# Bringing the attention sums of segments 1 to 3 to token-major layout by DMA transposes instead of selector matmuls, with a new instruction order

## The chip, the cores and the metric

The kernel runs on one core of a Trainium2 chip. The metric is the device time of one execution in microseconds (us), lower is better. The engines are named as the profile names them: PE is TensorE's matmuls, PEld its weight loads, DVE VectorE, ACT ScalarE, POOL GpSimd, SP SyncE (which issues the DMAs that matter here).

## The reference

One transformer block on 2048 tokens of width 640. The attention has 32 heads of 20 and goes through four segments of 512 tokens. Within a segment it is causal softmax attention; from one segment to the next it carries a linear memory M with its normaliser z. A SiLU feed-forward of width 1728 follows. All inputs are bf16.

```python
for s in range(4):                               # L = 512 tokens each
    p     = softmax(qs @ ks.T * scale + causal)  # per head
    a_dot = p @ vs
    a_mem = (phi(qs) @ M) / (phi(qs) @ z + 1e-6) # phi(t) = t+1 if t > 0 else exp(t)
    o     = g * a_mem + (1 - g) * a_dot          # g = sigmoid(beta), per head
    M, z  = M + phi(ks).T @ vs, z + phi(ks).sum()
h   = x + concat(o) @ wo                         # x was normalised before wq, wk, wv
out = h + silu(layernorm(h) @ w1) @ w2
```

## The kernel before

The kernel is a list of tasks. A task names its engines, what it reads and writes, and emits instructions. A long string ORDER, found by a search outside the kernel, lists every task in sequence with its engine (`/A`, `/D`, `/G` for ScalarE, VectorE, GpSimd) and its buffer slots (`:0,1`). Every engine runs its own tasks in that order.

Four heads form a group; one group in one segment is a tick, so segments 1 to 3 have 24 ticks (numbers 8 to 31). A tick goes: scores by row-tiled matmuls (`qk`), exponentials on ScalarE (`e`), causal masks on GpSimd (`mk`), sums by column-tiled matmuls (`av`), evacuation with the head's gate (`oe`), token-major layout and memory part on TensorE (`tn`), normalisation on VectorE (`nm`), and the addition of the two halves on GpSimd (`ad`).

```python
def e_mask(eng):                       # mk: GpSimd
    for co in diag:
        v = pt[:, pta.slot, :, co:co + 128]
        fns.append(lambda e, v=v: e.affine_select(out=v, in_=v, ..., compare_op=ALU.is_ge, fill=0.0, ...))
# ... (cut)
def e_av(eng):                         # av: sums of four heads, column-tiled; row 20 of 32 is the denominator
    ... e.matmul(bank(po)[32*r:32*r+32, q0:hi], lhsT=Vx[...], rhs=pt[...], tile_position=(0, 32*r))
def e_ot(eng):                         # oe: oTs = sums * (1 - g)-term, head-major [4 x 32 rows, 512 tokens]
    o, i_ = oTs[:, ots.slot, lo:hi], bank(po)[:, lo:hi]
# ... (cut)
pp = G.alloc("ps", 2 if s else 1)      # two PSUM banks: sums in the first, memory part in the second
def e_tn(eng):
    for i in range(b0, b1):            # memory part, token-major
        for q, (c, m) in enumerate(bl):
            ... e.matmul(bank(pp, 1)[:, V4*i:V4*i+V4], lhsT=phiQ[:, c, 128*i:128*i+128], rhs=Mzb[:, m, :], ...)
    for i in range(b0, b1):            # selector: turns 128 tokens of oTs token-major
        fns.append(lambda e, i=i: e.matmul(bank(pp)[:, V4*i:V4*i+V4],
                   lhsT=oTs[:, ots.slot, 128*i:128*i+128], rhs=sel, start=True, stop=True))
# ... (cut)
def e_nm(eng):                         # both halves at once, on VectorE
    T.add(DV, ... tensor_tensor(out=r2, in0=v[:, :, :, DH], in1=epsg, op=ALU.add))
    T.add(DV, ... reciprocal(out=r2, in_=r2))
    T.add(DV, ... tensor_tensor(out=on, in0=v[:, :, :, 0:DH], in1=r2, op=ALU.mult))      # 640 wide
def e_ad(eng):                         # ad: GpSimd adds the halves into otok
    T.add(PO, ... tensor_tensor(out=o_dst, in0=on[.., 0, :], in1=on[.., 1, :], op=ALU.add))
```

A rule of the program decides which full-tiled matmul tasks are split into four column tiles, so that they need no change of tiling:

```python
t.cm = t.mode == "c" or t.mode == "F" and (before + behind in ("cc", "cr", "rc"))
```

The softmax here doesn't subtract the row's maximum and nothing guards it: scores larger than these inputs give would overflow.

## Time and profile before

Three runs took a median of 304.71 us (304.3 to 306.35). The profiled execution has a span of 306.1 us and a mean granted clock of 0.989. The lines that carry the argument are shown in the prediction below.

| GpSimd work before | us |
|---|---|
| causal masks, 128 instructions of 0.65 us | 83.2 |
| additions of the halves, 24 of 0.81 us | 19.5 |
| powers for the layernorms, 32 of one column, 0.58 us each | 18.6 |
| memory products, 15 of 0.65 us | 9.6 |
| rest | 12.6 |
| all, 47% of the span | 143.5 |

A row of groups reads: line, engine, operation, output<-input, shapes, count, then busy us and mean ns of one, then the idle time of the engine ahead of it. The masks lie between exponentials and sums, so TensorE depends on GpSimd although GpSimd is idle half the time.

### The profile page before, as it was taken

The page shows a single profiled execution, that of the slowest core. Times are in us where ns is not written, and L with a number is a line of the kernel's source. Part 1 is how long each engine was busy: PE and PEld are TensorE (multiplying, and loading weights), DVE is VectorE, ACT ScalarE, POOL GpSimd, SP SyncE. Part 2 cuts the span into 40 slices and gives each one's busy share as a digit, 9 for nine tenths or more (in the row PEclk, how much of TensorE's full clock was granted, in tenths as well). Part 3 has the DMA queues.
Part 4 walks back from the last instruction along what each step waited for, and adds up shares of the span by engine and source line. Part 5 has one row for each costly group of instructions (what it writes and reads, how often), then busy time and mean ns, then how long its engine had stood idle before and what let it go on. Part 6 is the DMA issues. An engine that isn't in the chain of part 4 may idle for free.

```text
span 306.1 us, 8438 instructions
## 1 busy us (share of the span) xinstructions
PE 291.2 (95%) x3520; PEld 171.2 (56%) x3544; DVE 226.1 (74%) x496; ACT 220.0 (72%) x233; POOL 143.5 (47%) x280
## 2 busy tenths in 40 slices
PE   8989789999999999999999999999999999999996
PEld 6445435546665455576653544546665556764574
DVE  6677767898599896879998978886764696634623
ACT  4689959899989898995899798879768831003500
POOL 6145746375558766281736638464675530300000
PEclk9999879999999999999999999999999999999999
DMA  7949675660455111242433410144052014131002
GB/s 217 329 122 212 141 209 173 120 76 5 76 92 76 22 41 42 39 92 57 88 71 108 78 24 2 21 89 75 5 59 32 2 30 101 46 83 66 0 24 86
DMA packets 48581, 24.72 MB, mean 81 GB/s; under 512 B 38880, under 2 KB 47456, under 8 KB 48544
## 3 DMA queue, kind: packets, MB, share of 16 engines
q1 hardware_dynamic: 48544, 24.19, 35.5%
q8 instruction: 28, 0.46, 0.6%
q14 instruction: 9, 0.07, 0.1%
HBM read 10.41 MB, written 2.62 MB: 43 GB/s over the span
## 4 chain that ended last, share of the span: by engine, by line
PE 66%; DVE 14%; ACT 9%; DMA 6%; issue 3%; SPq 2%; ACTq 0%
PE ps_all L530 44%; PE ps_all L532 8%; PE ps_all L896 6%; PE ps_all L942 4%; DMA beta_bc<-in_A_beta_dram 4%; ACT PTA L907 3%; ACT PTB L907 2%; ACT PTE L907 2%; DMA x_tok<-in_A_x_dram 2%; DVE stt L720 2%; DVE on L1008 2%; PE ps_all L971 2%; DVE phiQ L849 1%; PE ps_all L975 1%; DVE sT L1176 1%
## 5 line engine op out<-in xcount | busy, mean ns | idle before, releaser
L907 ACT ACTIVATE PTA<-ps_all 128x2048 bf16<-128x2048 f32 x32 | 60.1, 1878 | 4.5 <-PE ps_all L896 4.2
L907 ACT ACTIVATE PTB<-ps_all 128x2048 bf16<-128x2048 f32 (+1 forms) x32 | 56.6, 1770 | 8.6 <-PE ps_all L896 8.5
L1170 ACT ACTIVATE th<-ps_all 128x512 f32<-128x512 f32 (+2 forms) x70 | 33.3, 501 | 39.0 <-PE ps_all L530 29.6
L919 POOL TENSOR_SCALAR_AFFINE_SELECT PTB<-PTB 128x512 bf16<-128x512 bf16 x64 | 41.3, 646 | 39.4 <-ACT PTB L907 37.1
L530 PE MATMUL ps_all<-w_sb,sT 128*128 128x320 bf16 x400 | 57.7, 299 | 0.5 <-DVE x_tok L1133 0.5
L530 PE MATMUL ps_all<-hT,w_sb 128*128 128x512 bf16 (+1 forms) x281 | 53.7, 338 | 1.1 <-DVE sT L1176 0.4
L1176 DVE SCALAR_TENSOR_TENSOR sT<-th,ps_all 128x512 bf16<-128x512 f32 (+2 forms) x70 | 37.8, 558 | 21.0 <-ACT th L1170 19.9
L530 PEld LDWEIGHTS ps_all<-w_sb,sT 128*128 128x128 bf16 x400 | 37.9, 98 | 17.6 <-issue 1.7
L530 PEld LDWEIGHTS ps_all<-hT,w_sb 128*128 128x128 bf16 x290 | 27.2, 98 | 22.9 <-issue 1.6
L907 ACT ACTIVATE PTE<-ps_all 128x2048 bf16<-128x2048 f32 (+1 forms) x20 | 34.1, 1707 | 6.4 <-PE ps_all L896 6.0
L919 POOL TENSOR_SCALAR_AFFINE_SELECT PTE<-PTE 128x512 bf16<-128x512 bf16 x40 | 26.2, 654 | 17.7 <-ACT PTE L907 16.3
L720 DVE BATCH_NORM_STATS2 stt<-x_tok 128x6 f32<-128x320 bf16 x64 | 27.8, 475 | 3.8 <-DMA x_tok<-in_A_x_dram 3.7
L1016 POOL TENSOR_TENSOR otok<-on 128x320 bf16<-128x320 bf16 x24 | 19.5, 812 | 18.7 <-DVE on L1008 18.7
L833 DVE CAST QK<-ps_all 128x512 bf16<-128x512 f32 x29 | 19.7, 686 | 8.8 <-PE ps_all L530 7.4
L1209 DVE SCALAR_TENSOR_TENSOR x_tok<-ps_all,x_tok 128x640 bf16<-128x640 f32 (+1 forms) x17 | 13.1, 780 | 12.8 <-PE ps_all L530 12.7
L896 PE MATMUL ps_all<-QK 20*128 20x256 bf16 (+3 forms) x360 | 20.5, 286 | 2.0 <-ACT PTE L907 1.3
L729 POOL TENSOR_TENSOR rst<-mvt,eps_c 128x1 f32<-128x1 f32 x32 | 6.5, 202 | 33.8 <-DVE mvt L723 33.8
L530 PE MATMUL ps_all<-xT,wqr 128*128 128x512 bf16 (+1 forms) x87 | 20.9, 368 | 0.9 <-issue 0.6
L919 POOL TENSOR_SCALAR_AFFINE_SELECT PTA<-PTA 128x512 bf16<-128x512 bf16 x24 | 15.7, 657 | 11.2 <-ACT PTA L907 10.9
L1008 DVE TENSOR_TENSOR on<-ps_all,rd 128x640 bf16<-128x640 f32 x24 | 19.8, 824 | 0.8
L530 PE MATMUL ps_all<-xT,wkr 128*128 128x512 bf16 x73 | 19.1, 394 | 1.1 <-issue 0.5
L731 POOL TENSOR_TENSOR rst<-rst,eps_c 128x1 f32<-128x1 f32 x32 | 18.6, 580 | 2.5
(92 smaller groups left out, 462.8 us busy)
## 6 DMA issues: line engine op xcount, KB each, us to landing
out_dram<-x_tok SPq DMA_DIRECT2D x15, 160.0 KB, 1.9
w_sb<-in_B_w_dram SPq DMA_DIRECT2D x5, 432.0 KB, 5.4
x_tok<-in_A_x_dram SPq DMA_DIRECT2D x3, 640.0 KB, 10.8
w_sb<-in_B_w_dram SPq DMA_DIRECT2D x3, 480.0 KB, 5.1
QKV<-QK SPq DMA_DIRECT2D x16, 72.0 KB
sT<-in_A_wq_dram SPq DMA_DIRECT2D x1, 800.0 KB, 5.9
sT<-in_A_wk_dram SPq DMA_DIRECT2D x1, 800.0 KB, 7.7
wv_sb<-in_A_wv_dram SPq DMA_DIRECT2D x1, 800.0 KB, 9.2
```

The lines of the kernel that those rows point to most:

```text
L530: return [lambda e: e.matmul(out(), lhsT=lhsT(), rhs=rhs(), start=start, stop=stop)]
L532: return [lambda e, r=r: e.matmul(out()[m * r:m * r + m, :], lhsT=lhsT()[:, m * r:m * r + m], rhs=rhs(), start=start, stop=stop, tile_posi ...
L720: T.add(DV, lambda e, hh=hh: e.bn_stats(out=stt[:, s, 6 * hh:6 * hh + 6], in_=xb[:, 320 * hh:320 * hh + 320]), reads=R((xa, xsub)), writes ...
L731: T.add(PO, lambda e: e.tensor_tensor(out=rst[:, s, :], in0=rst[:, s, :], in1=eps_c[:, 1:2], op=ALU.pow), reads=R((st, ["r"]), (C, ["half" ...
L833: (lambda e: e.tensor_copy(out=o, in_=i_))
L896: fns.append(lambda e, j=j, o=o, r=r, q0=q0, q1=q1, qa=qa, ka=ka: e.matmul(ps_all[:, o:o + q1 - q0], lhsT=ka[32 * r:32 * r + DH, 128 * j:1 ...
L907: T.add(AC, lambda e: e.activation(out=pt[:, pta.slot, q0:q0 + 4, 0:width], in_=sc3[:, b0:b0 + 4, 0:width], func=ACT.Exp, scale=SCALE), re ...
L919: fns.append(lambda e, v=v: e.affine_select(out=v, in_=v, pattern=[[0, 4], [1, 128]], compare_op=ALU.is_ge, fill=0.0, base=0, channel_mult ...
L1008: T.add(DV, lambda e: e.tensor_tensor(out=on[:, ona.slot, :, :].rearrange("p b (x e) -> p b x e", e=DH), in0=v[:, :, :, 0:DH], in1=r2.unsq ...
L1016: T.add(PO, lambda e: e.tensor_tensor(out=o_dst, in0=on[:, ona.slot, 0, :].rearrange("p (i x) -> p i x", i=4), in1=on[:, ona.slot, 1, :].r ...
L1170: T.add(AC, lambda e: e.activation(out=th[:, tha.slot, lo:hi], in_=bank(ps)[:, lo:hi], func=ACT.Tanh, scale=0.5), reads=R((ps, [0])), writ ...
L1176: T.add(DV, lambda e: e.scalar_tensor_tensor(out=sT[:, f, lo:hi], in0=th[:, tha.slot, lo:hi], scalar=1.0, in1=bank(ps)[:, lo:hi], op0=ALU. ...
```

## The change

The intent is to take 96 selector matmuls off TensorE, which is busy for 95% of the span. In segments 1 to 3 the evacuated sums go through a DMA transpose into a new tile `oto`. The memory part keeps one PSUM bank. The normalisation is halved, and the attention half becomes a task `nl` of its own: 13 of them are put on VectorE, 11 on GpSimd, which has no reciprocal task in this kernel and uses a power of -1. The column rule goes. ORDER is new throughout.

```diff
-            t.cm = t.mode == "c" or t.mode == "F" and (before + behind in ("cc", "cr", "rc"))
+            t.cm = t.mode == "c"
 ...
-            pp = G.alloc("ps", 2 if s else 1)
+            pp = G.alloc("ps", 1)
+            if s:
+                ota = G.alloc("oto")                                   # two buffers
+                dma(f"td{tag}", [(ots, [0])], [(ota, [0])],
+                    lambda e: e.dma_start_transpose(out=oto[:, ota.slot, :, :], in_=oTs[:, ots.slot, :]), ...)
 ...
-                for i in range(b0, b1):
-                    fns.append(... e.matmul(bank(pp)[...], lhsT=oTs[...], rhs=sel, ...))
+                    if not s:
+                        fns.append(... e.matmul(bank(pp)[...], lhsT=oTs[...], rhs=sel, ...))
 ...                                       # nm: the same three operations on the memory half only (16, 16, 320 wide)
+                def e_nl(eng):
+                    v = oto[:, ota.slot, :, :].rearrange("p i (r e) -> p (i r) e", e=32)
+                    if eng == DV:
+                        T.add(DV, lambda e: e.reciprocal(out=r2(0), in_=v[:, :, DH]), ...)
+                    else:
+                        T.add(PO, lambda e: e.tensor_tensor(out=r2(0), in0=v[:, :, DH],
+                                      in1=eps_c[:, 2:3].to_broadcast([128, 16]), op=ALU.pow), ...)
+                    T.add(eng, lambda e: e.tensor_tensor(out=o2(0), in0=v[:, :, 0:DH], in1=r2(0)..., op=ALU.mult), ...)
+                G.task(f"nl{tag}", {DV: 0.25 + dve_c(320), PO: 1.5}, e_nl, ...)
 ...
-zpad:0 mt1 mta1 iota mt3 halfc sel warm:0 mt2 mtb1 vpad0 x0:0 x1:1 ...      (ORDER, cut: some 90 lines)
+zpad:0 iota mt3 x0:0 x1:1 x2:2 x3:3 w_q:0 w_k w_wv:0 beta mt2 sel vpad0 ...
```

The number `PO: 1.5` is the duration in us that the program gives to the attention half on GpSimd.

## The prediction

> **What bounds the kernel now.** I read four views, in this order: the page's shares of the engines and its slices, the chain that ended last, the windows, and the matmul engine's timeline. First the shares, and the slices with the granted clock:
>
> ```profile
> PE 291.2 (95%) x3520; PEld 171.2 (56%) x3544; DVE 226.1 (74%) x496; ACT 220.0 (72%) x233; POOL 143.5 (47%) x280
> ...
> PE   8989789999999999999999999999999999999996
> ...
> PEclk9999879999999999999999999999999999999999
> ```
>
> TensorE is busy for 95% of the span; the two sevens and eights of its row are in slices 0 to 5, that is in segment 0, where the clock also dips. Then the chain:
>
> ```profile
> PE 66%; DVE 14%; ACT 9%; DMA 6%; issue 3%; SPq 2%; ACTq 0%
> ```
>
> Two thirds of it is TensorE, the rest short visits to other engines. So a matmul taken away counts nearly in full, and a microsecond on VectorE mostly doesn't. But busy time hides pauses, because the modelled ends of matmuls overlap. So I went to starts, in the timeline of TensorE:
>
> ```profile
> 146.02 0.39 PE L942 MATMUL ps_all<-PTB,Vx 128*32 128x384 bf16 x8
> 146.24 0.72 PE L532 MATMUL ps_all<-hT,w_sb 128*32 128x256 bf16 x20
> ...
> 151.54 0.31 PE L971 MATMUL ps_all<-Mzb,phiQ 128*128 128x84 bf16 x4
> 151.70 0.32 PE L975 MATMUL ps_all<-ident,oTs 128*128 128x84 bf16 x4
> 151.95 0.40 PE L896 MATMUL ps_all<-QK 20*128 20x384 bf16 x8
> 152.28 2.08 PE L530 MATMUL ps_all<-w_sb,sT 128*128 128x320 bf16 x14
> ```
>
> Three tilings alternate: full (128*128), column (128*32), row (20*128). Four memory matmuls start 0.16 us before the four selector matmuls behind them: 0.040 us each. The selectors then take 0.16 us, yet the row-tiled scores start only at 151.95, 0.09 us later: the price of a change of tiling. Column work followed by column work (146.02 to 146.24) pays nothing: (384+128)/2400 is 0.213 us. Over all 186 places where one matmul record and the next differ in tiling, the pause above streaming time has a median of 0.09 to 0.10 us, in each of the six directions.
>
> From this a budget of the 306.1 us profiled: streaming (columns at 2.4 GHz, four concurrent tiles counted once, small ones at 0.040) 263 us; 186 changes at 0.097, 18 us; 1.1 us before the first matmul and 3 us after the last; that leaves 21 us of waiting and half clock. By place, summing the excess between starts: about 3.4 us in the first 12 us, 7.9 between 12 and 60 (segment 0) and 10.7 in all the rest.
>
> **What the Trainium skill says.** "TensorE: Matmul & The Clock Gate", section "Back-to-back issue gap", gives N/2.4 + 2.5 ns between warm matmuls; the trace agrees, with a median of 2.5 ns above N/2.4 over 1,427 full-tiled pairs. "TensorEngine Tiling (Array Packing)", section "Key Properties", says that a change of tiling mode drains the engine; it states no price, the trace has 0.09 to 0.10 us. The first page's section "The HAM clock gate" says that an idle window of about 3.4 us halves the clock. The windows of one us each agree, with two half-clock stretches of 3.4 us:
>
> ```profile
> 35.00:36.00 1.00, 0.18 (x8) 0.00 (x0) 0.96 (x4) 1.00 (x2) 0.93 (x2) 0.88 0.53 97
> 36.00:37.00 1.00, 0.79 (x16) 0.56 (x20) 0.97 (x2) 1.00 (x2) 0.93 (x3) 0.50 0.55 104
> ...
> 43.00:44.00 1.00, 0.89 (x3) 0.34 (x3) 0.97 (x5) 1.00 (x1) 0.64 (x1) 0.50 1.04 379
> 44.00:45.00 1.00, 1.00 (x7) 0.16 (x9) 0.45 (x3) 0.72 (x2) 0.67 (x2) 0.50 1.07 394
> ```
>
> After window and length, the columns are the five engines, then the clock: 0.50 follows thin work. "DMA: Bandwidth & Descriptors", section "Anatomy of one DMA", says that a small transfer costs about 2 us, mostly completion; the page has 2.6 to 2.9 us from issue to landing for the transposes here.
>
> **The change part by part.** (a) In segments 1 to 3 the attention sum no longer goes through the selector. These rows tell the costs:
>
> ```profile
> L1008 DVE TENSOR_TENSOR on<-ps_all,rd 128x640 bf16<-128x640 f32 x24 | 19.8, 824 | 0.8
> ...
> L975 PE MATMUL ps_all<-ident,oTs 128*128 128x84 bf16 x128 | 11.4, 206 | 0.1
> ...
> L1007 DVE RECIPROCAL rd<-rd 128x32 f32<-128x32 f32 x24 | 8.5, 353 | 0.8
> ...
> L1002 DVE TENSOR_TENSOR rd<-ps_all,epsg 128x32 f32<-128x32 f32 x24 | 4.4, 184 | 7.8 <-PE ps_all L975 7.7
> ```
>
> Of the 128 selectors 32 belong to segment 0 and stay; 24 ticks of 4 go: 96 x 0.040 = 3.8 us of the bound. (The row's 206 ns is latency; 96 times that would be 20 us, and wrong.)
>
> (b) VectorE: a tick's normalisation was 184 + 353 + 824 = 1.36 us, 24 times 32.7 us. Half as wide it is, by my estimate from these rows and from the 320-wide PSUM read of 492 ns in the last block, 0.17 + 0.25 + 0.49 = 0.91 us, 21.8 us in all. The attention half is a new task, 13 times on VectorE at an estimated 0.25 + 0.43 us (8.8 us) and 11 times on GpSimd, whose power of one column takes 580 ns and whose 320-wide operation takes 812 ns in the trace: some 1.6 us each, 18 us. So VectorE falls by 2 us, GpSimd rises by 18 us to about 160.
>
> (c) SyncE issues 24 more transposes at about 1.25 us, 30 us on a queue that is now free for more than half of the span. In return the sum's second PSUM bank is free, and the memory matmuls no longer wait for the evacuation.
>
> (d) The rule that let a full matmul between two tiled tasks run as four column tiles is gone: 28 tasks had it. Counting tilings along the new order I get 214 changes against 186: 28 x 0.097 = 2.7 us more. This takes back most of (a). A full-tiled task itself streams at the same rate either way (ten of 320 columns take 1.37 us in both forms).
>
> (e) The new order of segment 0. It has 29 filler matmuls after the opening against 7: 2.4 us, meant for time when TensorE waits anyway. It should keep the clock up. A dip of 3.4 us costs at most 1.7 us. The first dip (36 to 39.4) is followed by a wait for the head copies until 40.4, so I count nothing for it; the second (42.6 to 46) is on the chain, 1.7 us. The warm-up of ScalarE moves from the empty start into the first scores, where 1.27 us may show.
>
> Sum: 304.7 - 3.8 + 2.7 - 1.7 = 301.9. I take another 1.2 us off for waits shortened by the free bank, the lighter VectorE and the search; this is a choice, some 6% of the 18.6 us of excess after the opening.
>
> **The rivals.** First, the exchange of tilings eats everything and segment 0 stays as it is: 304.7 - 3.8 + 2.7 = 303.6. For it: the changes are counted, while what the order gains is unknown. Second, the transposes make a new wait: evacuation, issue, 2.6 us, normalisation, addition in place of a matmul of 0.16 us; with two buffers each for the sums and their transposes, late ones hold the next evacuation and its PSUM bank. Against it: a tick comes only every 6 us or so, and the new order has nine other matmul tasks between the last sums and the last output projection. If it happened half a us in each of ten ticks, 306. Third, GpSimd becomes the bound where masks are dense: it is busy 5.6 of 6 us in one window already, though 47% on average; 1 to 3 us, 302 to 304. Fourth, waits and dips of segment 0 go almost wholly (up to 5 of its 7.9 us) and a quarter of the later 10.7 with them: 304.7 - 1.1 - 5 - 2.5 = 296.
>
> **Range and chances.** Predicted 300.7 us; 297.0 to 304.6 should hold it 8 times in 10. 2% faster is 298.6, which needs a gain of 6 us where the counted parts give 2.8; I give it 0.2. Slower by 2% needs the second rival at its worst: 0.03. Within 2%: 0.77.
>
> **What would show each step right or wrong.** The selector's row with 32 instances, not 128, and no column-tiled row of line 532. The pauses at changes of tiling summing to about 2.7 us more. A granted clock of 0.50 nowhere after the opening, or one stretch at most. Landing times of the new transposes near 2.7 us, and few waits of TensorE for evacuations of the sums. VectorE at about 224 us, GpSimd near 160. The prediction is wrong if the clock still dips, if the pauses don't grow by count, or if the excess in segments 1 to 3 moves by more than 3 us either way.

## The result

Three runs of the changed kernel took a median of 324.39 us (323.14 to 326.35). The ratio to before is 1.0639, with a 95% interval of 1.0535 to 1.0744. Ratios here are the mean time of one kernel's fast runs over that of the other's of the same rounds, so not quite the ratio of the medians. The kernel is 6.4% slower, outside the predicted range. The profiled spans are 322.2 and 306.1 us, with granted clocks of 0.984 and 0.989.

The page of the changed kernel: shares of the engines, TensorE by slices, granted clock by slices, chain that ended last.

```profile
PE 293.1 (91%) x2867; PEld 166.4 (52%) x2891; DVE 219.7 (68%) x523; ACT 219.3 (68%) x232; POOL 182.1 (57%) x303
...
PE   7899888999999498799989999699998979999996
...
PEclk9999999999999879999999999899999999999999
...
PE 52%; POOL 21%; DVE 10%; DMA 7%; ACT 6%; issue 3%; SPq 1%; ACTq 0%; DVEq 0%; POOLq 0%
```

VectorE fell by 6 us. GpSimd rose by 38.6 us, more than twice what was expected, and it holds 21% of the chain, in which it had no entry before. Apart from the last slice, TensorE's row has its lowest values in slices 13 and 25 (counted from 0), in segments 1 and 2, and the clock dips there and just behind. In segment 0 the clock has no dip left in this profile.

The groups of instructions, with shapes kept apart:

```profile
L1029 POOL TENSOR_TENSOR rd<-oto,eps_c 128x16 f32<-128x16 bf16 x11 | 32.1, 2916 | 0.0
...
L734 POOL TENSOR_TENSOR rst<-rst,eps_c 128x1 f32<-128x1 f32 x32 | 18.0, 564 | 2.5
...
L1017 DVE TENSOR_TENSOR on<-ps_all,rd 128x320 bf16<-128x320 f32 x24 | 11.8, 491 | 4.7 <-POOL otok L1039 4.0
...
L1032 POOL TENSOR_TENSOR on<-oto,rd 128x320 bf16<-128x320 bf16 x11 | 8.0, 727 | 0.9
...
L984 PE MATMUL ps_all<-ident,oTs 128*128 128x84 bf16 x32 | 3.6, 209 | 0.0
```

The first two rows are the same operation, a power (of -1 from bf16 in the first, of -0.5 from f32 in the second). One column takes 564 ns; sixteen columns take 2916 ns. The attention half on GpSimd is therefore 2.916 + 0.727 = 3.64 us, and eleven of them 40 us. The last row is the selector of segment 0, with its 32 instances.

Next the timeline of TensorE in the first bad place (start, duration, then in brackets the idle time before and the releaser):

```profile
106.17 0.33 PE L980 MATMUL ps_all<-Mzb,phiQ 128*128 128x84 bf16 x4
106.33 1.24 PE L532 MATMUL ps_all<-xT,wqr 128*128 128x512 bf16 x5
107.41 0.32 PE L980 MATMUL ps_all<-Mzb,phiQ 128*128 128x84 bf16 x4
112.03 0.62 PE L945 MATMUL ps_all<-PTA,Vx 128*32 128x512 bf16 x4 [4.30 <-DVE phiQ L849]
```

TensorE stands still for 4.30 us ahead of a tick's sums, and then runs them at half clock: 0.62 us for four tiles of 512 columns, where 0.40 us was usual a little earlier. The profile names a VectorE operation as the releaser. By the program these sums read Vx and the masked exponentials, and no phiQ. So I looked at the chain in that stretch (start, duration, what):

```profile
99.56 2.95 POOL rd L1029
102.52 0.07 issue
102.58 0.73 POOL on L1032
103.31 0.55 POOL Mzb L1123
103.86 0.79 POOL PTE L922
...
105.33 2.88 POOL rd L1029
...
108.28 0.73 POOL on L1032
109.01 0.74 POOL otok L1039
109.75 0.60 POOL PTB L922
...
111.04 1.48 POOL PTA L922 x2
```

GpSimd works without a gap: a power, a product, a memory product, masks, another power, product, addition, and only then the masks of PTB and PTA. These are what the waiting sums read. Of the two PTA masks only the first is of this tick: by the view of tile PTA it starts at 111.0 and takes 0.885 us, so it ends at about 111.9, and the weight load of the waiting sums starts at 112.00 (the second mask is of the next tick). The exponentials of this PTA had left ScalarE by 105.57. The windows, first of before, then of after, put the engines side by side; after window and length come PE, PEld, DVE, ACT, POOL, the clock, the DMA share and GB/s:

```profile
108.00:114.00 6.00, 5.69 (x80) 3.11 (x70) 5.93 (x11) 5.38 (x6) 3.62 (x7) 1.00 0.19 52
```

```profile
108.00:114.00 6.00, 1.97 (x25) 0.80 (x26) 3.50 (x8) 0.75 (x3) 5.78 (x10) 0.73 0.13 26
114.00:120.00 6.00, 5.78 (x39) 3.24 (x42) 2.49 (x6) 3.78 (x3) 5.92 (x7) 0.70 0.11 22
```

In the stretch from 108 to 114, TensorE falls from 5.69 to 1.97 us of work, ScalarE from 5.38 to 0.75 and VectorE from 5.93 to 3.50, while GpSimd rises from 3.62 to 5.78 of 6. A second place is at 204 us, with a wait of 3.10 us before 206.63. There the chain goes through two powers and the additions behind them to VectorE's normalisation, which TensorE waits for, and not through masks.

### The profile page after: what moved, and what is told of

Same layout as the page of the kernel before. It is cut to its first block, busy times and chain, and to the rows that moved or that the text cites. A ratio compares the mean times of both kernels' runs of the same rounds, so it can differ in the third digit from the quotient of the medians.

```text
span 322.2 us, 7230 instructions
## 1 busy us (share of the span) xinstructions
PE 293.1 (91%) x2867; PEld 166.4 (52%) x2891; DVE 219.7 (68%) x523; ACT 219.3 (68%) x232; POOL 182.1 (57%) x303
## 4 chain that ended last, share of the span: by engine, by line
PE 52%; POOL 21%; DVE 10%; DMA 7%; ACT 6%; issue 3%; SPq 1%; ACTq 0%; DVEq 0%; POOLq 0%
PE ps_all L532 42%; POOL rd L1029 9%; PE ps_all L899 5%; POOL PTB L922 3%; PE ps_all L945 3%; DMA oT<-otok 3%; POOL otok L1039 3%; DMA sT<-in_A_wk_dram 3%; POOL on L1032 2%; POOL PTA L922 2%; ACT PTB L910 2%; DVE on L1032 1%; ACT PTE L910 1%; DVE sT L1199 1%; DMA QKV<-QK 1%
## 5 line engine op out<-in xcount | busy, mean ns | idle before, releaser
L532 PE MATMUL ps_all<-w_sb,sT 128*128 128x320 bf16 x448 | 65.0, 299 | 0.8 <-DVE sT L1199 0.8
L532 PE MATMUL ps_all<-hT,w_sb 128*128 128x512 bf16 (+1 forms) x314 | 60.9, 335 | 3.0 <-DVE on L1017 1.5
L532 PEld LDWEIGHTS ps_all<-w_sb,sT 128*128 128x128 bf16 x448 | 42.6, 98 | 20.2 <-issue 2.0
L532 PEld LDWEIGHTS ps_all<-hT,w_sb 128*128 128x128 bf16 x325 | 29.5, 98 | 27.0 <-issue 2.6
L1029 POOL TENSOR_TENSOR rd<-oto,eps_c 128x16 f32<-128x16 bf16 x11 | 32.1, 2916 | 0.0
L532 PE MATMUL ps_all<-xT,wkr 128*128 128x512 bf16 x94 | 24.6, 398 | 4.2 <-DVE on L1017 3.1
L836 DVE CAST QK<-ps_all 128x512 bf16<-128x512 f32 (+1 forms) x30 | 19.9, 665 | 9.4 <-PE ps_all L532 9.2
L532 PE MATMUL ps_all<-wv_sb,xT 128*128 128x320 bf16 x160 | 26.1, 314 | 0.2
L532 PE MATMUL ps_all<-wo_sb,oT 128*128 128x320 bf16 x160 | 23.9, 300 | 2.0 <-DVE phiK L849 1.2
L945 PE MATMUL ps_all<-PTA,Vx 128*32 128x512 bf16 (+1 forms) x160 | 13.1, 350 | 9.5 <-DVE phiQ L849 4.3
```

The lines of the kernel that those rows point to most:

```text
L532: return [lambda e: e.matmul(out(), lhsT=lhsT(), rhs=rhs(), start=start, stop=stop)]
L836: (lambda e: e.tensor_copy(out=o, in_=i_))
L945: fns.append(lambda e, j=j, r=r, h=h, pa=pa, pt=pt, co=co, q0=q0, ji=ji: e.matmul(bank(po)[32 * r:32 * r + 32, q0:hi], lhsT=Vx[:, vx.slot, ...
L1029: T.add(PO, lambda e: e.tensor_tensor(out=r2(0), in0=v[:, :, DH], in1=eps_c[:, 2:3].to_broadcast([128, 16]), op=ALU.pow), reads=R((ota, [0 ...
```

## The experiments

Seventeen runs were made of sixteen kernels (one ran twice), in five calls; each call has its own runs of before, with medians of 306.84, 306.31, 306.11, 305.92 and 306.58 us. These are 1 to 2 us above the 304.71 that forecasts in us were worked out from, so ratios are what to compare. The theory: the power on GpSimd is the cause, by its length and by what queues behind it. The rivals: the detour of the sums through the DMA; the lost column rule; and the new order itself.

### Which part of the attention half

**All attention halves on VectorE.** Only the engine letter in ORDER changes, 11 times.

```diff
-nl8/G:0,0 nm8 mb02:0 mk12e v20:6 e12b0:1 nl9/G:1,1 ...
+nl8/D:0,0 nm8 mb02:0 mk12e v20:6 e12b0:1 nl9/D:1,1 ...
```

> The changed kernel with all 24 attention halves (reciprocal and product) on VectorE; the eleven powers of GpSimd are gone, the order is the same. Theory P (the power of 16 columns on GpSimd takes 2.91 us, not the 0.58 us of one column, and holds up masks and sums behind it): GpSimd falls by 11 x (2.91 + 0.73) = 40 us to about 142, VectorE rises by 11 x 0.74 = 8 us, no wait of TensorE over 2 us after segment 0, and the time comes to 301 to 306 us. Rival D (the detour through the DMA transposes is itself the new wait): the long waits stay and the time stays within 3 us of 324. Rival T (more changes of tiling, or the new order as such): the same, 320 or more.

Correct; median 315.96 us, ratio 1.0306 (1.0267 to 1.0345). VectorE rises to 228.6 us busy and 17% of the chain, GpSimd falls to 145.0. Half of the loss is gone, the other half is not, and neither forecast held (301 to 306 us for the power, 320 or more for the rivals). That the halves now wait in VectorE's queue, and other work behind them, would fit, but no run isolates it.

**A multiplication in place of the power.** Wrong results; the same operands, the same place.

```diff
-    in1=eps_c[:, 2:3].to_broadcast([128, 16]), op=ALU.pow),
+    in1=eps_c[:, 2:3].to_broadcast([128, 16]), op=ALU.mult),
```

> The changed kernel with a multiplication in place of the power, on the same engine, place and shape; the values come out wrong on purpose. Theory P: the 16-column instruction falls from 2.91 us to about 0.25, GpSimd by 11 x 2.65 = 29 us to about 153, and the time to 302 to 307 us: it is the function, not the place, that costs. If GpSimd is too slow for these halves whatever the function (rival G), the time stays above 312. Rivals D and T: within 3 us of 324.

Median 308.87 us, ratio 1.0084 (1.0039 to 1.0129). From 1.0639, this is 5.5 points, some 17 us, from one operation code in eleven instructions. Its shares, and the row of `oto` with minimum, median and maximum in ns:

```profile
PE 292.8 (95%) x2891; PEld 165.8 (54%) x2891; DVE 222.9 (72%) x523; ACT 219.7 (71%) x232; POOL 154.1 (50%) x303
```

```profile
L1029 POOL TENSOR_TENSOR rd<-oto,eps_c x11: 213/220/229, 99.2 to 243.1; 128x16 f32<-128x16 bf16 x11
```

In the changed kernel the same row reads:

```profile
L1029 POOL TENSOR_TENSOR rd<-oto,eps_c x11: 2899/2907/2995, 99.5 to 254.1; 128x16 f32<-128x16 bf16 x11
```

The multiplication takes 0.220 us where the power has a median of 2.907, and GpSimd's share of the chain falls from 21% to 1%. So it is neither the width nor the strided bf16 input that costs, but the power. In this trace the sums that waited until 112.03 start at 107.15, with 0.8 us of the difference already there at the tick before (100.34 against 101.12), and in the window at 108 all engines are busy again:

```profile
108.00:114.00 6.00, 4.95 (x48) 2.76 (x44) 5.83 (x13) 5.07 (x5) 5.41 (x10) 1.00 0.52 49
```

**The reciprocal on VectorE, the product where it was.** A correct kernel without the power.

```diff
+ def e_nr(eng):   # new task nr, VectorE
+     T.add(DV, lambda e: e.reciprocal(out=r2(0), in_=v[:, :, DH]), ...)
- nl11/G:3,1
+ nr11:3 nl11/G:1
```

> The changed kernel with all 24 reciprocals on VectorE and the eleven products left on GpSimd; results are right. Theory P: like the multiplication for the power, 302 to 307 us, with GpSimd at about 182 - 32 = 150 us and VectorE 11 x 0.25 = 3 us up. Rivals D and T: within 3 us of 324.

Correct; 311.54 us, ratio 1.0178 (1.0127 to 1.0228). **The same kernel again**, on another chip, as a base for others:

> The kernel of the run with reciprocals on VectorE, word for word, measured again with more rounds, as the measure for the two runs that were built on it (tilings back: 1.0228; no fillers: 1.0240). If it comes to 1.016 to 1.020, both edits made it slower by about 0.5%; if it comes to 1.022 or more, neither did anything.

Correct; 312.85 us, ratio 1.0227 (1.0182 to 1.0271). Both times are above the forecast of 302 to 307 us, also when it is moved up by the 1 to 2 us by which before ran slower here. This is the best correct form of the changed program that I found, and still slower than before. It is a point or so above the multiplication; that GpSimd's products now wait for VectorE's queue would fit, but no run isolates it.

**Two powers of 8 columns.** Is the cost per instruction or per column?

```diff
+ for q in range(2):
+     T.add(PO, ... tensor_tensor(out=r2(0)[:, 8*q:8*q+8], in0=v[:, 8*q:8*q+8, DH], in1=..[128, 8], op=ALU.pow))
```

> The changed kernel with each power of 16 columns cut into two of 8. If the power costs by column (a line through 0.565 us for 1 column and 2.907 for 16: 0.41 + 0.156 a column), one of 8 takes 1.66 us and the span grows by up to 11 x 0.4 us, to 322 to 328. If it costs by instruction, each takes 2.9 us and the span is 335 us or more. If columns are handled in groups of 16, 2.9 us each too.

Correct; one time of 333.07 us, state unknown, so the time decides nothing. The row does:

```profile
L1030 POOL TENSOR_TENSOR rd<-oto,eps_c x22: 1632/1640/1731, 100.9 to 264.1; 128x8 f32<-128x8 bf16 x22
```

8 columns take 1.640 us and 16 take 2.907: 0.158 us a column and 0.37 us once. That puts one column at 0.53 us; 0.564 is measured, for the power of -0.5 from f32. A line of 0.41 + 0.156 per column meets all three to 0.02 us.

### The detour through the DMA

**No wait for the transposes.** On top of the multiplication, the halves read a constant tile of ones; the transposes are still issued. Wrong results.

```diff
-                    v = oto[:, ota.slot, :, :].rearrange("p i (r e) -> p (i r) e", e=32)
+                    v = ones[:, :, :].rearrange("p i (r e) -> p (i r) e", e=32)
```

> The kernel with a multiplication for the power (1.0084 of before), whose attention halves read a tile of ones in place of the transposed sums; the transposes are still issued, but no engine waits for their data. Values are wrong on purpose. Rival D (what is left of the loss is waiting for the 24 transposes): 0.985 to 0.998 of before. Theory O (what is left is the new order itself, with its changes of tiling and fillers): 1.004 to 1.012, as without the edit.

307.91 us, ratio 1.0057 (1.0015 to 1.01), against 1.0084 with the wait. The intervals overlap: in the new order the wait costs 0.8 us at most likely, and perhaps nothing. In the changed kernel the transposes land in a median of 2.5 us.

**The old order with the change in it.** Before, with its ORDER and its column rule; the transpose is put right behind the evacuation, the halves on VectorE ahead of the additions, four buffers for `oto`.

```diff
-mzc8 ad9 mb03:0 h2_1_2 av11:3 qk13a0:4 oe11/A:0 h2_1_3 ... oe10/D:1
+mzc8 nl9/D ad9 mb03:0 h2_1_2 av11:3 qk13a0:4 oe11/A:0 td11:3 h2_1_3 ... oe10/D:1 td10:2
```

> The order and the tiling rule of the kernel before, with only the token-major attention sum: transposes right behind the evacuations, reciprocal and product of all 24 ticks on VectorE just ahead of the addition, four buffers for the transposed sums. TensorE loses 96 selectors (3.8 us), VectorE gains 24 x (0.74 - 0.46) = 6.8 us. Theory P+order (the power and the new order made the loss; the idea is sound): 0.985 to 0.998 of before. Rival D (the detour itself costs): VectorE stands still for transposes and the ratio is 1.01 or more.

Correct; 363.07 us, ratio 1.1851 (1.1796 to 1.1906). A far larger loss than expected. **The same with the products on GpSimd** (`nl9/D` becomes `nr9 nl9/G`):

> Like the old order with the token-major sum, but with all 24 products on GpSimd (0.73 us each, 17.5 us) and only the reciprocals (0.25 us) on VectorE, which so loses 24 x (1.36 - 0.91 - 0.25) = 5 us. Theory P+order: 0.985 to 1.000 of before, and better than all on VectorE if VectorE is what the short waits of TensorE are for. Rival G (GpSimd too full, masks wait behind products): 1.01 or more.

Correct; 362.87 us, ratio 1.1855 (1.1802 to 1.1909). Which of the two engines does the products makes no difference here. The waits of SyncE in the first of the two (line waited for, us in total, times, longest) led on:

```profile
SPq L971 <- ACT oTs L959: 32.4, 6, 11.6
SPq L971 <- DVE oTs L961: 31.1, 4, 14.2
```

SyncE stands for 63.5 us with a transpose in hand whose evacuation has not come. Its timeline shows what that holds up:

```profile
242.49 1.21 SPq L1141 DMA_TRANSPOSE oT<-otok  x1
253.19 1.19 SPq L971 DMA_TRANSPOSE oto<-oTs  x1
254.43 1.41 SPq L864 DMA_DIRECT2D QKV<-QK  x2
255.88 2.51 SPq L1080 DMA_TRANSPOSE phiKt<-phiK  x2
258.44 2.82 SPq L864 DMA_DIRECT2D QKV<-QK  x4
```

From 243.70 to 253.19 nothing is issued; then one transpose of sums, and behind it eight other transfers in one go. They belong to other work: head copies for the scores, transposes for the memory. The transposes of the output (`oT`) are issued from the same queue; in one line of the program alone the matmuls of this trace wait 11.8 us for them and the weight loads 12.8.

**The old order, transposes later.** Each `td` is moved some ten tasks back, with its halves and additions.

```diff
-... oe10/D:1 td10:2 o1 qk12a0:4 e12a0:1 tn10:0 qe200/D:0 v20:2 qk12b0:4 mb04:0 mk13a mk12a nm10:2,0 ...
+... oe10/D:1 o1 qk12a0:4 e12a0:1 tn10:0 qe200/D:0 td11:2 v20:2 qk12b0:4 mb04:0 mk13a mk12a td10:3 nm10:2,0 ...
```

> The old order with the token-major sum on VectorE (1.185 of before), with one edit: each of the 24 transposes stands about ten tasks later in SyncE's queue, and the half and the addition later where they stood within 20 tasks of it. Theory H (SyncE's queue is in order, and a transpose that waits for its evacuation holds up the head copies and the transposes of the output behind it): SyncE's waits at the new transposes fall from over 60 us to under 30, TensorE's waits for transposed outputs from 24 us to under 6, and the ratio to 0.99 to 1.06. If the old order can't take the detour for another reason (buffers, VectorE standing still): above 1.12.

Correct; 340.78 us, ratio 1.1134 (1.1082 to 1.1186). The later place of 24 issues in one queue, with the halves and additions that moved along, is worth 7 points, 22 us; the run does not part the two. The result lies between the forecast for the queue (0.99 to 1.06) and the one for another reason (above 1.12). SyncE's waits for evacuations fell to 36.0 us, not under 30:

```profile
SPq L970 <- ACT oTs L958: 24.2, 5, 10.3
...
SPq L970 <- DVE oTs L960: 11.8, 3, 5.1
```

The other 11 points stay open; the old order was searched for other tasks, and I did not take them apart.

### The column rule

**Before without the rule.**

```diff
-            t.cm = t.mode == "c" or t.mode == "F" and (before + behind in ("cc", "cr", "rc"))
+            t.cm = t.mode == "c"
```

> The kernel before with only one part of the change: full matmuls between tiled tasks no longer run as four column tiles. Counted along its order, the changes of tiling go from 186 to 217. Theory P with the price read from the trace: 31 x 0.097 = 3.0 us more, 307 to 308.5 us. Rival T (the tiling rule is what made the changed kernel slow): 315 us or more. If pauses hide behind waits that are there anyway: under 306.

Correct; 308.26 us, ratio 1.0055 (1.002 to 1.009): 1.7 us, where 31 more changes at 0.097 us would give 3.0.

**The rule put back** into the reciprocal kernel (201 changes of tiling against 214):

> The kernel of the run with reciprocals on VectorE, with one more edit: the old rule of tilings is back, 13 full tasks of the new order run as four column tiles, and the counted changes of tiling go from 214 to 201. The rule alone, taken from the kernel before, cost 1.7 us for 31 counted changes (0.055 each). Theory: 0.7 to 1.3 us faster than that run, a ratio to before of 1.013 to 1.016. If tilings are free in the new order because other waits cover them: 1.017 to 1.019.

Correct; 312.88 us, ratio 1.0228 (1.0193 to 1.0264), the same as the base of 1.0178 and 1.0227. **The rule put back** into the kernel without power and waits:

> The kernel without power and without waits for transposes (1.0057 of before), with the old rule of tilings back: 201 counted changes of tiling in place of 214. If each change costs its 0.097 us where TensorE is the bound, 1.3 us come off: 1.000 to 1.003. If the rule is worth nothing in this order, as on the kernel with reciprocals on VectorE (1.0228 against 1.0227): 1.004 to 1.008.

307.98 us, ratio 1.0078 (1.0027 to 1.0129), against 1.0057. Nothing gained, in either.

### Selectors, fillers, warm-up

**Before with one selector per tick.** What are selector matmuls worth? 72 of the 96 go, nothing else. Wrong results.

```diff
-                for i in range(b0, b1):
+                for i in range(b0, b0 + 1 if s else b1):
```

> The kernel before with one selector matmul in place of four in each of the 24 ticks of segments 1 to 3: 72 of the 96 that the change removes are gone, nothing else moves; values are wrong on purpose. If a matmul taken off TensorE counts nearly in full, as I predicted, 72 x 0.040 = 2.9 us come off, a ratio of 0.990 (0.988 to 0.993). If short waits take the room, 0.995 to 1.000.

305.38 us, ratio 0.997 (0.9928 to 1.0012). Counted in full it would be 72 x 0.040 = 2.9 us, a ratio of 0.990, below the interval. Measured are 0.9 us.

**The 29 fillers taken out** (matmuls on a tile of zeros, meant for idle time) of the reciprocal kernel (`fill5`, `fill1`, `fill12`, `fill7`, `fill3`, `fill1` leave ORDER), and then of the kernel without power and waits:

> The kernel of the run with reciprocals on VectorE, without the 29 filler matmuls of segment 0 after the opening. Theory F (the fillers stand in the way, since TensorE's idle time there was not where they are): 1 to 2.5 us faster than that run, a ratio of 1.010 to 1.015, the granted clock 0.50 at most once in segment 0. Rival: without them the clock falls to half for one or two stretches of 3.4 us and the ratio is 1.018 to 1.028.

> The same kernel (1.0057 of before) without the 29 fillers of segment 0 after the opening. If the fillers stand on TensorE's path, up to 29 x 0.109 = 3.2 us come off: 0.996 to 1.002. If they fill idle time and hold the clock up: 1.004 or more, with one more half-clock stretch in segment 0.

313.47 us, ratio 1.024 (1.0195 to 1.0284), and 308.3 us, 1.0081 (1.0032 to 1.013): no difference from their bases in either. In each of the four profiles, with and without fillers, the clock of segment 0 is low in one slice; without them it is at 6 tenths instead of 7 in one pair and equal in the other. One profile each is too few to build on.

**Both, rule back and fillers out:**

> Both edits on the same kernel (1.0057 of before). If both count as I counted them in the prediction (1.3 us for the tilings, 2.4 us for the fillers), 0.993 to 0.998, and only then would the new order without its power be better than the one before; if neither counts, 1.003 to 1.008.

309.71 us, ratio 1.0116 (1.0072 to 1.0159): nothing gained; the interval still overlaps that of the base, 1.0015 to 1.01.

**The warm-up of ScalarE back at the start** (`warm:0` moves from behind the first scores to the second place in ORDER):

> The kernel without power and without waits for transposes (1.0057 of before), with ScalarE's warm-up activation (1.26 us) moved back from 14.2 us, just ahead of the first exponential, to the empty start. If it delays segment 0 where ScalarE sets the pace, up to 1.3 us come off: 1.001 to 1.004. If ScalarE had that time to spare (it waits 0.27 us for TensorE just behind): 1.004 to 1.009.

308.7 us, ratio 1.0068 (1.0031 to 1.0106), the same as 1.0057. No part of what is left of the loss has been found by these runs.

## Why the prediction was wrong

The predicted ratio was 0.987, the measured one 1.064. By the steps of the prediction:

- **The step that failed is the size of one term in part (b):** "11 times on GpSimd, whose power of one column takes 580 ns and whose 320-wide operation takes 812 ns in the trace: some 1.6 us each, 18 us." The product was right at 0.73 us. The power was carried over from one column to sixteen; it takes 2.91 us, so the eleven halves are 40 us and not 18. (The two durations quoted add up to 1.39 us; nothing shown makes 1.6 of them.) The program carries nearly the same figure, 1.5 us, in its own table. GpSimd went to 182.1 us instead of "about 160".
- **The third rival was right in kind and wrong in size.** "GpSimd becomes the bound where masks are dense" is what happened, but I gave it 1 to 3 us, because my halves were short. With 2.9 us instead of 0.2 in eleven places the ratio goes from 1.0084 to 1.0639. This is shown. That the masks behind the powers carry it to TensorE is read from the chain, the windows and the sums that come 4.9 us sooner without the power (0.8 of it was there a tick before); at 204 us it is additions and VectorE that carry it. The power is not all that was missed: without it, at 1.0084, the kernel would still lie above the predicted range, whose upper end is 304.6 / 304.7, a ratio of 1.000.
- **Part (a), "a matmul taken away counts nearly in full", failed on a small scale.** 2.9 us of selectors taken away gave 0.9 us (at most 2.2 by the interval). TensorE busy for 95% is not yet TensorE bound at every instant.
- **Part (d) was right on the price and wrong on its effect.** Pauses at changes of tiling have medians of 0.091 to 0.102 us in all six directions after the change too, and 214 changes are there as counted. But taking the rule from before cost 1.7 us and not 3.0, and putting it back into two variants of the changed kernel gave nothing. That other engines catch up during the pauses would explain it; no run shows it.
- **Part (c): the queue is free, but not free of order.** By sum, 24 issues fit. In the new order the detour costs some 0.8 us, within the noise, so the second rival was small in the changed kernel. In the old order the change without the power cost 18.5 points, of which later issues, halves and additions gave 7 back.
- **Part (e): no gain came from segment 0.** By the budget of the prediction, a count of starts that no view shows, the excess between 12 and 60 us fell from 7.9 to 6.4 us, while the 22 added fillers took 2.4 us. Removing all 29 changed nothing measurable. The two dips of before are gone from the one profile of the changed kernel, but the order of segment 0 is not shown to have done it: the reciprocal kernel, measured again, has the same order there and a dip in slice 5, while before with one selector per tick has the old order and no dip. Nor do the windows bear out an idle stretch of 3.4 us ahead of a dip, as the prediction read them. Ahead of the first dip TensorE was busy for 0.82, 0.98, 0.66 and 0.18 of four windows of 1 us (32 to 36), ahead of the second for 0.34, 0.61, 0.99 and 0.72 (39 to 43). Only the length of the dips agrees.
- **The "another 1.2 us off" for waits and the search was a choice, and nothing supports it.** Without power and without waits for transposes, the new order stands at 1.0057, not 0.987. Neither the column rule nor the fillers nor the warm-up accounts for it. With selectors at a third of their count and no gain in segment 0 much of the gap to 0.987 would close, but the runs don't add it up. It stays open.

In its reading of the first lines the prediction counts TensorE's row loosely: it has one seven and three eights in slices 0 to 5. Of the signs of being right named in advance, these came: 32 selectors, no column-tiled row of line 532, 2.5 us to landing, VectorE at 219.7 (224 predicted; the three normalising operations 0.166 + 0.253 + 0.491 = 0.91 us as estimated). GpSimd and the clock (two stretches at half after segment 0, of 6.8 and 3.4 us) said no, and so did the excess in segments 1 to 3, which was not to move by more than 3 us: the span grew by 16.1 us, and not in segment 0.

## What to carry to other kernels

Take the duration of a new instruction from a row of the same operation and the same width, or measure it alone first: the duration of one column was no guide to that of sixteen here. When work is moved to an engine that is half idle, ask what stands behind it in that engine's order and who waits for that; here masks worth 0.65 us each stood behind powers of 2.9 us. The same holds for the issuing queue of DMAs: put an issue where its operand is ready, since one that waits holds up the issues behind it (9.5 us, with eight transfers behind, in the old order).

## What the Trainium skill lacked or had wrong

- "GPSIMD Engine Reference", section "3.1 Elementwise — side-by-side cycle accounting", gives one figure for `tensor_tensor`, measured for an add, and none by operation. Here a `tensor_tensor` of 128x16 on GpSimd takes 0.220 us as a multiplication and 2.907 us as a power; the power follows 0.41 us + 0.156 us a column (0.564, 1.640 and 2.907 us at 1, 8 and 16 columns, the first a power of another exponent and input type).
- "TensorEngine Tiling (Array Packing)", section "Key Properties", says that a change of tiling drains the engine and gives no price. Both traces have 0.09 to 0.10 us in each of the six directions between full, column and row tiling; and taking 31 of them in costs 1.7 us (0.6 to 2.8 by the interval), not 3.0.
- "DMA: Bandwidth & Descriptors", section "Issuing engines are not separate DMA queues", says that issuing from several engines only saves the sequencer's time to issue, "which is usually small". It does not speak of an issue that waits for its operand; elsewhere the page places such a wait on the issuing sequencer, but gives no price for the issues behind it. Here SyncE stood for 9.5 us ahead of one transpose with eight transfers of other work behind it, 63.5 us in a run, and moving these issues later, with the halves and additions, gave 22 us back. Issuing them from another engine was not tried.
